# A sketched-attention and Fourier-mixing kernel: rows folded fourfold, a rearranged last group and a new instruction order

## The chip, the cores and the metric

The kernel runs on one core of a Trainium2 chip. The metric is the device time of one execution in microseconds (us); lower is better. Five engines work from queues of their own and meet only at semaphores: TensorE (PE, matmuls, with a separate row PEld for its weight loads), VectorE (DVE), ScalarE (ACT), GpSimd (POOL) and SyncE (SP, which issues nearly all transfers between memory and the core).

## The reference, cut to what matters

Two parts follow each other. The first is linear attention with a polynomial sketch for 4 batches, 4 heads, 1088 rows and a head width of 32:

```
phi(x) = (S1 x) outer (S2 x)            # 8 x 8 = 64 features
kv = sum over rows of phi(k) * v ;  z = sum over rows of phi(k)
x  = (phi(q) kv) / (phi(q) z + 1e-6)    # heads side by side: 1088 rows of 128
```

The second mixes the result with a Fourier transform and a small network:

```
u   = x + real(fft over 128 columns of fft over 1088 rows of x)
un  = (u - mean) / sqrt(var + 1e-6)     # per row
out = u + relu(un @ w_ch1) @ w_ch2      # 128 -> 512 -> 128, output float32
```

## The kernel before, in words

**Steps and order.** The kernel is a list of named steps. Each has an engine, the tiles it reads and writes, and its banks of the accumulator memory (PSUM, eight banks of 512 floats per partition). The string `ORDER` writes out by hand in which order all steps are issued, and so the order on every engine's queue. `ENGINE` moves single steps to another engine than their default, `FILL` puts matmuls on zeros ahead of a step, `BEHIND` lets a load wait for an earlier load, `AFTER` makes one step wait for another, and `BANK` gives each use its bank.

**Attention, per batch b.** `ld_k`, `ld_v` and `ld_q` load. `kT` and `qT` transpose blocks of 32 on DVE. `kpr` (L361) projects k on PE, `kab` copies on ACT, `kp` multiplies to features on POOL or DVE, `vc` copies v, `kv` (L395) sums features times v on PE, and `kvz` copies the result to SBUF. For the query, `qf` (L435) projects on PE in two halves, `qa` (ACT) and `qp` (DVE, L446) make the features, `pnd` (L481) multiplies with `kvz`, and `den`, `rden`, `x` (L490 to L496) divide. The 64 rows per head beyond 1024 go through small tiles of their own (`kt_`, `qt_`, `vt`).

**The row transform, per batch.** Partition p and slots 0 to 7 of `x{b}` hold four consecutive rows of each half of the sequence, and slot 8 holds the leftover rows. `dfold` adds and subtracts column c and column 128 - c. `fold` adds and subtracts the two halves of the sequence. `srow` (L521) multiplies with tables of cosines and sines (`tab`, `tabl`, made from phases on POOL and DVE by `turn`, `rest`, `size` and on ACT by sine), in five groups of six matmuls. `zev` takes the half spectrum out of PSUM, `zrev` makes the mirrored half with signs, `zlast` picks the columns of the leftover rows.

**The mixer, per group g of 512 rows.** Groups 0, 1, 2, 3, 5, 6, 7 and 8 are main groups, two per batch; 4 and 9 hold the leftover rows of two batches each. `mix` (L574, L577) adds x and the column transform in PSUM. `bn` and `var` take the variance on DVE, `sd` (L612) its root on ACT, `rc` the reciprocal, `un` (L623) the scaled rows. `xt` (L635) transposes them by a transfer for groups 0 to 6, and `tr` and `ut` do so through PE and a copy for 7 to 9. `ph` (L643) is the hidden layer in two halves, `rl` (L650 on ACT, L652 on DVE) the relu, `po` (L657) the second layer, summed onto u in the same bank. `fin` copies to SBUF and `out` stores. Group 8 (`TWO`) is spread over two banks and stored in two halves.

Of the kernel before, what the change touches and what calls it, by code (L numbers as in the profile page):

```python
# [12 lines left out]
I32 = mybir.dt.int32  # L13
# [9 lines left out]
LAST = HALF - 512  # L23
QD = DM // 2
NK = HALF // 2 + 1
NB = NK // 2 + 1
BY_DMA = (0, 1, 2, 3, 4, 5, 6)
SPLIT = {}
TURNS = {"un": 5, "unT": 5, "ht": 3, "ot": 4, "st": 5, "sm": 5}
NXD = 1  # L30
WARM = 4
TWO = 8
MAGIC = float(1.5 * 2 ** 23)
# [23 lines left out]
def program(nc, T, x, bank):  # L57
# [82 lines left out]
    def ld_q(b, half):  # L140
        return [nc.sync.dma_start(view(T(f"q_in{b % 3}"), 4 * H * D * half, [[4 * D, H], [1, 4 * D]], p, n),  # L141
                                  dram(x["q"], (b * H * S + half * HALF + 4 * p) * D, [[4 * D, n], [S * D, H], [1, 4 * D]]))
                for p, n in parts(f"ld_q{b}.{half}", 128)]

    def ld_qt():

        return [nc.sync.dma_start(view(T("qt_in"), 0, [[D, B * H], [1, D]], 32 * par + 16 * half, 16),  # L147
                                  dram(x["q"], (512 + HALF * half + par) * D, [[2 * D, 16], [S * D, B * H], [1, D]]))
                for par in range(2) for half in range(2)]
# [31 lines left out]
    def c_iota():  # L181
        first = nc.gpsimd.iota(T("pi")[:], pattern=[[0, 1]], base=0, channel_multiplier=1)

        nc.gpsimd.iota(T("sr")[:], pattern=[[1, 6]], base=0, channel_multiplier=4,
                       allow_small_or_imprecise_dtypes=True)
        return first
    add("c_iota", POOL, "", "iota", c_iota)

    def c_kk():
# [55 lines left out]
    add("t_cos1", ACTE, "phb/1 phb/2 phb/3 tabsin", "tab/C1", lambda: sin(
        view(T("tab"), 2 * W, [[4 * W, 2], [NB, 2], [1, NB]]), view(T("ph"), 2 * W + NB - 2, [[W, 2], [NB + 1, 2], [-1, NB]]), S))
# [24 lines left out]
    def d_trig():  # L271
        for c in range(2):
            lo, hi = slice(QD * c, QD * c + QD), slice(QD - QD * c, 2 * QD - QD * c)
            nc.scalar.activation(out=T("wd")[lo, c, :], in_=T("dpm")[lo, :], func=ACT.Sin, scale=-2 * PI / DM, bias=T("hpi")[lo, 0:1])
            nc.scalar.activation(out=T("wd")[hi, c, :], in_=T("dph")[hi, :], func=ACT.Sin, scale=-2 * PI / DM)
    add("d_trig", ACTE, "dphb dpm hpi tabsin", "wd0", d_trig)

    def d_alt(engine):

        done = []  # L280
        for c in range(2):
            p = QD - QD * c
            for i in range(2):
                done.append(memset(engine, view(T("wd"), DM * c + i, [[2, QD]], p, 1), 1.0 - 2 * i))
# [617 lines left out]
```

## Time and profile before

| what | value |
|---|---|
| median of 3 runs | 82.4 us (82.08 to 84.12) |
| the profiled execution | 82.32 us |
| its span in the profile | 80.4 us |
| busy PE, DVE, ACT, POOL | 69.6, 65.0, 49.5, 45.2 us |
| granted PE clock | 1.00 |
| read and written | 7.22 MB and 2.23 MB |

The span runs from the first to the last recorded work; the profiled execution's own time is 1.92 us longer. A busy share is a mean over stages with different limits, so the table of busy time by stage and the chain of work that ended last are read beside it. Idle time of an engine that sets nothing costs nothing.

### The profile page before, as it was taken

The numbers are of one execution on the slowest core, as the hardware profiler recorded it, in microseconds if no ns is written. First come the engines' busy times: TensorE is split into PE (matmuls) and PEld (weight loads), VectorE is DVE, ScalarE is ACT, GpSimd is POOL, SyncE is SP. The second block draws the span as 40 slices with busy tenths as digits, with TensorE's granted clock in tenths as the row PEclk, the third lists the DMA queues.
The fourth block names the chain that finished last, engine by engine and source line by source line (L and its number), as shares of the span: only waits on it lengthen the run. The fifth ranks groups of instructions, "written<-read, shape, count | busy, mean of one in ns | idle before, by whom it ended". The sixth has DMA issues, their size and how long they took to land.

```text
span 80.4 us, 3294 instructions
## 1 busy us (share of the span) xinstructions
PE 69.6 (87%) x1368; PEld 52.0 (65%) x1375; DVE 65.0 (81%) x178; ACT 49.5 (62%) x85; POOL 45.2 (56%) x84
## 2 busy tenths in 40 slices
PE   4998693799999999999999999989997969797930
PEld 2323552489799766878788789956674837583720
DVE  5895879999869999999759699999878659894800
ACT  6244576475693645479692285609978548979530
POOL 6888579975857499597999619149850010000000
PEclk9999999999999999999999999999999999999999
DMA  0969998379929659556015003030500466133042
GB/s 8 270 174 269 229 288 208 53 208 229 227 44 310 207 144 292 151 125 212 0 34 43 0 8 65 8 65 0 177 19 16 95 190 253 29 130 138 24 176 90
DMA packets 16095, 10.47 MB, mean 130 GB/s; under 512 B 6864, under 2 KB 14544, under 8 KB 16080
## 3 DMA queue, kind: packets, MB, share of 16 engines
q1 hardware_dynamic: 15896, 10.13, 47.0%
q8 instruction: 10, 0.16, 0.8%
q10 hardware_dynamic: 184, 0.14, 0.5%
q14 instruction: 5, 0.04, 0.2%
HBM read 7.22 MB, written 2.23 MB: 117 GB/s over the span
## 4 chain that ended last, share of the span: by engine, by line
PE 48%; DVE 18%; DMA 11%; SPq 8%; ACT 7%; issue 4%; DVEq 0%; ACTq 0%
PE ps L481 9%; PE ps L395 8%; PE ps L435 7%; PE ps L657 6%; DMA t_qt_in<-in_q_dram 6%; PE ps L643 5%; DMA t_unT__166<-t_un__161 5%; PE ps L361 4%; SPq L141 3%; ACT t_ht__168 L650 3%; PE ps L521 2%; PE ps L458 2%; SPq L147 2%; DVE t_x__130 L496 2%; DVE t_x__131 L496 2%
## 5 line engine op out<-in xcount | busy, mean ns | idle before, releaser
L102 POOL TENSOR_TENSOR t_kp__119<-t_ab__117 128x512 f32<-128x512 f32 x7 | 7.3, 1068 | 1.5 <-ACT t_ab__117 L413 1.1
L650 ACT ACTIVATE t_ht__167<-ps 128x1024 bf16<-128x1024 f32 x6 | 6.0, 1022 | 1.6 <-PE ps L481 1.6
L102 POOL TENSOR_TENSOR t_kp__118<-t_ab__116 128x512 f32<-128x512 f32 x6 | 6.3, 1069 | 1.0 <-ACT t_ab__116 L413 1.0
L442 ACT COPY t_qa__122<-ps 128x1024 f32<-128x1024 f32 x4 | 4.1, 1013 | 3.1 <-DVE t_qp__124 L446 1.9
L650 ACT ACTIVATE t_ht__168<-ps 128x1024 bf16<-128x1024 f32 x4 | 4.1, 1024 | 2.9 <-PE ps L577 1.9
L442 ACT COPY t_qa__123<-ps 128x1024 f32<-128x1024 f32 x4 | 4.1, 1014 | 2.3 <-PE ps L435 2.3
L643 PEld LDWEIGHTS <-t_w1b 128*128 128x128 bf16 x40 | 3.0, 97 | 3.7 <-issue 1.5
L90 PE MATMUL ps<-t_wz 128*128 128x512 bf16 x12 | 5.0, 526 | 0.0
L481 PEld LDWEIGHTS ps<-t_kvz,t_qp__124 128*64 128x64 f32 x128 | 4.0, 137 | 0.9 <-ACT t_kvz L95 0.4
L481 PE MATMUL ps<-t_kvz,t_qp__124 128*64 128x66 f32 x128 | 4.4, 223 | 0.1
L395 PE MATMUL ps<-t_v__121,t_kp__119 128*64 128x33 f32 x128 | 4.3, 223 | 0.1
L102 POOL TENSOR_TENSOR t_eo__133<-t_xd__132 128x516 bf16<-128x516 bf16 x4 | 4.2, 1052 | 0.4 <-DVE t_xd__132 L102 0.3
L395 PEld LDWEIGHTS ps<-t_v__121,t_kp__119 128*64 128x64 f32 x128 | 4.1, 138 | 0.4 <-POOL t_zl__143 L96 0.4
L395 PE MATMUL ps<-t_v__120,t_kp__118 128*64 128x33 f32 x128 | 4.3, 223 | 0.0
L481 PEld LDWEIGHTS ps<-t_kvz,t_qp__125 128*64 128x64 f32 x128 | 3.9, 137 | 0.5 <-issue 0.4
L481 PE MATMUL ps<-t_kvz,t_qp__125 128*64 128x66 f32 x128 | 4.2, 223 | 0.0
L395 PEld LDWEIGHTS ps<-t_v__120,t_kp__118 128*64 128x64 f32 x128 | 4.1, 138 | 0.1
L650 ACT ACTIVATE t_ht__169<-ps 128x1024 bf16<-128x1024 f32 x4 | 4.0, 1027 | 0.0
L652 DVE TENSOR_SCALAR t_ht__168<-ps 128x1024 bf16<-128x1024 f32 x2 | 2.5, 1225 | 1.7 <-PE ps L657 1.0
L435 PE MATMUL ps<-t_qT__115,t_sa 32*64 32x256 f32 x64 | 2.8, 400 | 1.2 <-DVE t_qp__124 L446 1.2
L379 DVE STREAM_TRANSPOSE t_kT__112<-t_k_in__105 128x512 f32<-128x512 f32 (+1 forms) x3 | 2.7, 886 | 1.1 <-DMA t_k_in__105<-in_k_dram 1.1
L361 PE MATMUL ps<-t_sblk,t_kT__112 128*64 128x64 f32 x64 | 2.5, 226 | 1.1 <-DVE t_kT__112 L379 1.1
(266 smaller groups left out, 216.6 us busy)
## 6 DMA issues: line engine op xcount, KB each, us to landing
t_q_in__109<-in_q_dram SPq DMA_DIRECT2D x4, 256.0 KB, 3.3
t_v_in__107<-in_v_dram SPq DMA_DIRECT2D x8, 128.0 KB, 3.6
t_k_in__106<-in_k_dram SPq DMA_DIRECT2D x2, 512.0 KB
t_v_in__108<-in_v_dram SPq DMA_DIRECT2D x8, 128.0 KB, 3.3
t_k_in__105<-in_k_dram SPq DMA_DIRECT2D x2, 256.0 KB
t_q_in__110<-in_q_dram SPq DMA_DIRECT2D x2, 256.0 KB, 6.6
t_q_in__111<-in_q_dram SPq DMA_DIRECT2D x2, 256.0 KB
t_k_in__105<-in_k_dram SPq DMA_DIRECT2D x1, 512.0 KB
```

The lines of the kernel that those rows point to most:

```text
L90: nc.tensor.matmul(T("ps")[:, free, :], w[:, 0:128], bass.AP(tensor=w.tensor, offset=w.offset, ap=[list(w.ap[0]), [0, 4], [1, 128]]), star ...
L102: return (nc.vector if engine == DVE else nc.gpsimd).tensor_tensor(out=out, in0=in0, in1=in1, op=op)
L361: nc.tensor.matmul(ps(use, 64 * t, [[1, 64]], 64 * c, 64), view(src, 128 * t + 64 * c, [[1, 64]]), T("sblk")[:], start=True, stop=True, ti ...
L379: nc.vector.transpose(view(T(f"kT{b % 2}"), 128 * lo, [[1, 128 * n]]), view(T(f"k_in{b % 2}"), D * lo, [[D, n], [8 * D, 4], [1, D]]))
L395: nc.tensor.matmul(ps(f"kv{b}", 33 * pr, [[1, 33]], 64 * c, 64), kp, v, start=(t == 0), stop=(t == 8), tile_position=(0, 64 * c), skip_gro ...
L435: nc.tensor.matmul(ps(f"q{b}.{pr}", 512 * g + 256 * w, [[1, 256]], 64 * h, 64), view(T(src), 0, [[1, F]], 32 * g, 32), view(T(f"qT{b % 2}" ...
L442: nc.scalar.copy(T(f"qa{pr}")[:], ps(f"q{b}.{pr}", 0, [[512, 4], [1, 256]]))
L481: nc.tensor.matmul(ps(f"nd{b}", 512 * (s // 3) + 132 * (s % 3) + 66 * pr, [[1, 66]], 64 * c, 64), w, view(T("kvz"), 132 * b + 66 * pr, [[1 ...
L496: nc.vector.tensor_tensor(out=view(T(f"x{b}"), 0, [[384, 3], [32, 12], [1, 32]]), in0=ps(f"nd{b}", 0, [[512, 3], [33, 12], [1, 32]]), in1= ...
L643: nc.tensor.matmul(ps(use, 128 * n * i, [[1, 128 * n]]), T("w1b")[:, 128 * c:128 * c + 128], own("unT", g)[:, 0:128 * n], start=True, stop ...
L650: nc.scalar.activation(out=out, in_=in_, func=ACT.Relu)
L657: nc.tensor.matmul(ps(u, ut_at(g, t), [[1, 128]]), view(own("ht", g), (128 if g % 5 == 4 else 512) * c + 128 * t, [[1, 128]]), T("w2b")[:, ...
```

## The change

The rows are laid out anew: partition p of a half holds two neighbouring rows, and partitions 64 to 127 of a q load start 288 rows further on. Even and odd slots hold rows that mirror each other about the middle of the sequence, so a new step `mfold` adds and subtracts them before `dfold`, and `dfold` and `fold` work on half as many slots. `srow` then needs three groups of six matmuls. To get the mirrored order, the query projection reads its columns in another, partly reversed order, and the mixer uses a reversed identity (`jdb`) and a table with signs (`wd` with a second half, made by `d_neg`). Two phase tables are made in place of four; ACT mirrors them (`t_far`). A main group is stored as two blocks of 256 rows with 1 KB per packet.

Group 8 (`LATE`) is no longer scaled ahead of its hidden layer: `un8` copies u as it is, `uc8` keeps u in float32, `po8` starts banks of its own, and `fin8` multiplies its sum by the reciprocal deviation and adds u. (A positive scale per row can be taken through the relu.) Order, engines, fillers, added waits and banks are new throughout.

```diff
-TURNS = {"un": 5, "unT": 5, "ht": 3, "ot": 4, "st": 5, "sm": 5}
+TURNS = {"un": 5, "unT": 5, "ht": 3, "ot": 4, "st": 5, "sm": 5, "uc": 1}
+LATE = (8,)
+FINE = ()
...
     def ld_q(b, half):
-        return [nc.sync.dma_start(view(T(f"q_in{b % 3}"), 4 * H * D * half, [[4 * D, H], [1, 4 * D]], p, n),
-                                  dram(x["q"], (b * H * S + half * HALF + 4 * p) * D, [[4 * D, n], [S * D, H], [1, 4 * D]]))
-                for p, n in parts(f"ld_q{b}.{half}", 128)]
+        return [nc.sync.dma_start(view(T(f"q_in{b % 3}"), 4 * H * D * half, [[4 * D, H], [1, 4 * D]], 64 * far, 64),
+                                  dram(x["q"], (b * H * S + half * HALF + (FAR if far else 1)) * D,
+                                       [[4 * D, 64], [S * D, H], [1, 4 * D]])) for far in range(2)]
...
-    for i, t in enumerate((0, 2, 1, 3)):
+    for a in range(2):
+        add(f"t_turn{a}", POOL, "rows kk", f"pha/{a}", lambda a=a: turn(T("ph")[:, a, :], a, base(), S))
+        add(f"t_ph{a}", DVE, f"pha/{a} rows", f"phb/{a}", lambda a=a: rest(T("ph")[:, a, :], a, base()))
...
-    add("t_neg", eng("t_neg", DVE), "tab/S0 tab/S1 tab/C0 tab/C1", "neg", lambda: t_neg(eng("t_neg", DVE)))
...
+    def c_x9(e):
+        return [memset(e, T(f"x{b}")[:, 9, :], 0.0) for b in range(B)][0]
...
     def qfeat(b, pr):
...
-                        view(T(f"qT{b % 2}"), 128 * (2 * pr + h), [[512, 2], [1, 128]], 32 * g, 32),
+                        view(T(f"qT{b % 2}"), 128 * (2 * pr + h) + (127 if g > 1 else 0),
+                             [[512, 2]] + [[-s if g > 1 else s, n] for s, n in ((32, 2), (1, 32), (64, 2))], 32 * g, 32),
...
+    def mfold(b, engine, w):
+        X = T(f"x{b}")
+        return tt(engine, view(T(f"xm{b % NXM}"), 5 * DM * w, [[DM, 5], [1, DM]]), view(X, 0, [[2 * DM, 5], [1, DM]]),
+                  view(X, DM, [[2 * DM, 5], [1, DM]]), (ALU.add, ALU.subtract)[w])
...
     def fold(b, engine, w):
-        return tt(engine, view(T(f"eo{b % 3}"), 12 * QD * w, [[3 * QD, 4], [1, n]]), view(X, 0, [[n, 4], [1, n]]), view(X, 4 * n, [[n, 4], [1, n]]), (ALU.add, ALU.subtract)[w])
+        return tt(engine, view(T(f"eo{b % 3}"), 6 * QD * w, [[3 * QD, 2], [1, n]]), view(X, 0, [[n, 2], [1, n]]), view(X, 2 * n, [[n, 2], [1, n]]), (ALU.add, ALU.subtract)[w])
     def srow(b):
...
-        for t in range(4):
+        for a in range(2):
+            six(lambda c, part: view(T(f"eo{b % 3}"), 6 * QD * c + 3 * QD * a + QD * part, [[1, QD]]),
...
+    def zev(b, half, engine):
+        copy(engine, view(T(f"z{b}"), 256 * half, [[128, 2], [1, 128]]),
+             ps(f"z{b}", *((512, [[-511, 2], [1, 128]]) if half == 0 else (783, [[-512, 2], [-1, 128]]))))
     def zrev(b, engine):
+        return copy(engine, view(T(f"z{b}"), 512, [[128, 4], [1, 128]]), view(T(f"z{b}"), 127, [[128, 4], [-1, 128]]))
...
     def un(u, g, n, engine):
+        if g in LATE:
+            copy(engine, view(out, 0, [[1, 128 * n]]), ps(u, 0, [[1, 128 * n]]))
+            return
...
     def fin(u, g, lo, hi, engine):
+        if g in LATE:
+            for t in range(lo, hi):
+                nc.vector.scalar_tensor_tensor(
+                    out=own("ot", g)[:, 128 * t:128 * t + 128], in0=ps(u, 128 * (t - lo), [[1, 128]]), scalar=own("sm", g)[:, t:t + 1],
+                    in1=own("uc", g)[:, 128 * t:128 * t + 128], op0=ALU.mult, op1=ALU.add)
+            return
...
+    def st(b, half, g, ws):
+        row = ((1, HALF + 1), (HALF + FAR, FAR))[half]
+        w, n = ws[0], len(ws)
+        return [(nc.sync, nc.scalar)[g == TWO and w == 1].dma_start(
+            dram(x["out"], (b * S + row[w]) * DM, [[2 * DM, 128], [(row[1] - row[0]) * DM, n], [1, 2 * DM]]),
+            view(own("ot", g), 256 * w, [[256, n], [1, 256]]))]
...
+    "c_v11": "DVE", "c_eo2": "DVE", "c_mask": "DVE", "c_vt0": "DVE", "c_sgn": "DVE", "vc0": "DVE", "t_far1": "ACT",
+    "t_far0": "ACT", "vc1": "ACT", "mf0.1": "DVE", "den1": "ACT", "kp2.3": "DVE", "vc2": "ACT", "vc3": "ACT", "w2b":
+    "ACT", "kp3.0": "DVE", "mf2.1": "DVE", "fin0": "ACT", "un4": "ACT", "un2": "ACT", "mf3.0": "DVE", "df3.1": "DVE",
+    "fin1": "ACT", "fin4": "ACT", "var6": "POOL", "z3.0": "DVE", "un8": "ACT", "var8": "POOL", "var7": "POOL", "ut9":
+    "DVE", "ut8": "DVE", "fin5": "ACT", "rl9.0": "DVE", "ut7": "DVE", "rl8.1": "DVE", "fin9": "ACT", "rl7.0": "DVE",
+    "fin6": "ACT", "rl8.0": "DVE", "fin7": "ACT",
...
-    "warm": (1, 1, 6), "qf0.1": (0, 2, 6), "qf0.0": (0, 3, 6), "kpr1": (0, 1, 7), "po8.0": (0, 1, 0),
+    "s_t": (0, 2, 0), "kpr0.1": (1, 1, 0), "qf0.1": (0, 1, 0), "qf1.0": (0, 2, 5), "kpr1": (1, 0, 3), "pnd0": (0, 2,
+    3), "pnd1": (0, 2, 0),
...
+    "t_turn1": "d_pm", "kp0.2": "t_pm", "kp1.3": "vc0", "kp1.2": "l_pm", "df0.1": "mf0.1", "mf2.0": "mf2.1", "mf3.1":
+    "mf3.0", "df3.0": "df3.1",
...
+c_wz warm ld_k0.0 c_bias c_v11 c_eo2 a_sin c_id ld_s1 ld_s2 s_t c_x9 c_iota c_mask c_kk c_rows c_more c_vt0 c_idb
+c_xd0 ld_k0.1 t_turn0 kT0.0 c_sgn c_cen c_jdb d_turn d_ph d_pm ld_q0.1 kT0.1 s_use kpr0.1 ld_q0.0 c_qtp kpr0.0 d_trig
...
+out4 bn8 mix7 uc8 po3 rc9 un9 ph5.1 rl5.1 var8 bn7 var7 fin3 tr9 ut9 out3 sd7 tr8 ut8 rc7 un7 ph9.0 ph6.0 rl6.0 po5
+fin5 tr7 ph8.1 rl9.0 po9 ut7 ph6.1 rl8.1 fin9 ph7.0 rl6.1 ph7.1 ph8.0 po6 rl7.0 out9 sd8 rl7.1 po7 fin6 rc8 rl8.0
+po8.0 fin8.0 po8.1 fin7 out5 out6 out7 fin8.1 out8.0 out8.1
```

More of the change, by code (lines that the diff above doesn't have):

```diff
@@ L22 @@
 ROWS = S // 32
[L23 removed]
+FAR = 288
 QD = DM // 2
@@ L858 @@
-rl0.0 bn2 var2 pnd3 eo2.0 sd2 rc2 s2 den3 rden3 x3 un2 z2 mix3 ph1.0 bn3 xt2 var3 po0 fin0 out0 rl1.0 sd3 ph1.1 ph2.0
-rc3 un3 rl1.1 rl2.0 df3.0 zr2 df3.1 eo3.1 mix5 bn5 var5 zl2 ph2.1 rl2.1 po1 mix4 eo3.0 mix6 bn4 var4 sd5 po2 sd4 rc5
-fin1 fin2 xt3 ph3.0 rl3.0 rc4 un4 un5 xt4 ph3.1 bn6 var6 sd6 rc6 xt5 un6 s3 z3 xt6 rl3.1 ph4.0 po3 zr3 rl4.0 ph5.0
-rl5.0 po4 fin3 zl3 ph5.1 fin4 mix9 bn9 mix7 ph6.0 var9 rl5.1 sd9 bn7 out2 out3 out1 out4 rl6.0 var7 rc9 po5 un9 ph6.1
-sd7 fin5 rc7 mix8 rl6.1 tr9 un7 ut9 ph9.0 tr7 rl9.0 po6 bn8 var8 ut7 sd8 rc8 fin6 ph7.0 rl7.0 un8 po9 out5 ph7.1 rl7.1
@@ L863 @@
[L863 removed]
+c_wz warm ld_k0.0 c_bias c_v11 c_eo2 a_sin c_id ld_s1 ld_s2 s_t c_x9 c_iota c_mask c_kk c_rows c_more c_vt0 c_idb
+c_xd0 ld_k0.1 t_turn0 kT0.0 c_sgn c_cen c_jdb d_turn d_ph d_pm ld_q0.1 kT0.1 s_use kpr0.1 ld_q0.0 c_qtp kpr0.0 d_trig
+qT0.1 ld_kt t_turn1 l_turn ld_q1.1 ld_vt0 qT0.0 ld_q1.0 t_ph0 ld_k1 t_ph1 t_pm ld_qt c_vt1 ld_v0.0 ld_v0.2 ld_v0.1
+ld_v0.3 kab0 kp0.2 ld_vt1 qf0.1 ld_v1.0 kt_T c_eo0 qa0.1 qT1.1 qf0.0 qa0.0 ld_q2.0 kp0.1 c_eo1 qp0.1 kt_pr kt_ab qT1.0
@@ new lines @@
+w1c zl0 kpr3 qp2.0 vc2 kab3 kp3.2 kp3.1 qf3.0 bn0 var0 sd0 kp3.3 mf1.0 kv2 df1.0 qa3.0 rc0 un0 w1b xt0 qp3.0 mix1 bn1
+var1 kvz2 vc3 w2b eo1.0 pnd2 kp3.0 den2 ph0.0 rden2 sd1 rc1 x2 kv3 eo1.1 ph0.1 un1 mf2.1 rl0.0 s1 mf2.0 rl0.1 kvz3
+z1.1 z1.0 zr1 po0 fin0 zl1 mix4 bn4 var4 sd4 mix2 xt1 bn2 var2 sd2 rc4 un4 xt4 pnd3 df2.0 df2.1 eo2.0 eo2.1 ph1.1 rc2
+rl1.1 un2 ph1.0 rl1.0 den3 rden3 x3 mix3 s2 mf3.0 z2.0 bn3 var3 sd3 ph4.0 mf3.1 df3.1 zl2 xt2 rc3 un3 po1 z2.1 mix5
+bn5 df3.0 rl4.0 po4 ph2.0 out0 xt3 zr2 eo3.1 fin1 fin4 mix6 var5 rl2.0 eo3.0 sd5 bn6 ph2.1 rc5 un5 out1 var6 rl2.1 s3
```

325 lines of the change are left out of this document (171 added, 154 removed).

## The prediction

> **What bounds the kernel now.** I read the page's busy shares first, then the chain that ended last, then a table of busy time by stage, cut where that chain changes its engine, and last the timeline of the end.
>
> The page's first part says that no engine is full over the whole span, and that TensorE (PE) and VectorE (DVE) are closest:
>
> ```profile
> PE 69.6 (87%) x1368; PEld 52.0 (65%) x1375; DVE 65.0 (81%) x178; ACT 49.5 (62%) x85; POOL 45.2 (56%) x84
> ```
>
> The table by stage (start:end, length, busy us of PE, PEld, DVE, ACT, POOL, clock, DMA share, GB/s) shows five different limits:
>
> ```profile
> 0.00:15.17 15.17, 11.15 (x149) 5.10 (x150) 12.04 (x39) 7.36 (x14) 12.17 (x35) 1.00 0.80 195
> 15.17:40.32 25.15, 25.00 (x686) 20.71 (x688) 23.25 (x38) 16.82 (x28) 19.03 (x30) 1.00 0.62 174
> 40.32:53.15 12.83, 12.17 (x287) 10.75 (x289) 11.09 (x33) 7.14 (x14) 7.73 (x11) 1.00 0.17 25
> 53.15:65.24 12.09, 10.50 (x129) 7.90 (x131) 9.73 (x40) 8.92 (x14) 6.30 (x10) 1.00 0.29 69
> 65.24:77.14 11.90, 10.76 (x117) 7.50 (x119) 8.89 (x31) 8.86 (x14) 0.00 (x0) 1.00 0.34 123
> 77.14:80.40 3.26, 0.00 (x0) 0.00 (x0) 0.00 (x0) 0.37 (x1) 0.00 (x0) 1.00 0.46 161
> ```
>
> Until 15.2 us loads and constants set the pace. From 15.2 to 40.3 PE is full (25.00 of 25.15). From 40.3 to 53.2 the chain goes qa2.0, qp2.0, pnd2, den2, x2, den3, x3, mostly on DVE. Then it goes through normalisation and a transposing DMA, and from 65.2 through PE, ACT and DVE in turn. The granted clock is 1.00 everywhere. The chain itself (start, length, engine, what, line):
>
> ```profile
> 31.44 1.08 PE ps L361 x32
> 32.52 1.76 PE ps L521 x30
> 34.29 1.05 PE ps L435 x32
> ...
> 45.74 1.37 DVE t_x__130 L496
> ...
> 61.13 4.07 DMA t_unT__166<-t_un__161
> ...
> 73.37 0.44 DVE t_unT__164 L96
> 73.80 0.05 issue
> 73.85 1.10 PE ps L643 x4
> 74.95 0.89 PE ps L657 x16
> 75.84 0.22 PE ps L90
> 76.06 0.01 issue
> 76.06 1.08 PE ps L657 x16
> 77.14 0.02 issue
> 77.17 0.37 ACT t_ot__173 L95
> ```
>
> The reader is to see that only the first sequence transform (L521 at 32.52) lies on the chain; the other three ran under the waits at 40.3, 51.1 and 61.1. At the end PE waits for the last group's normalised rows (0.44 on DVE) before its last hidden layer.
>
> **The change part by part.** The profiled execution took 82.32 us with a span of 80.4, so 1.92 lie around it; it is 0.08 under the median of 82.4.
>
> *The transform (srow).* 30 matmuls become 18 per batch of the same width. 1.76/30 is 0.059 us each, so 0.70 per batch and 2.8 of PE work in all. Counted: the first, 0.70; the other 2.1 go into waits that the chain has anyhow, and come back only if PE binds there. The leftover rows' mixL issues 2 matmuls fewer each (0.05 each by "0.20 x4" in the chain): 0.1. A zero matmul at 75.84 goes, but four new ones stand before pnd0 and pnd1 (0.22 to 0.32 each); they run while ACT copies kvz (two of 0.21), which pnd has to wait for; without that cover they cost 1.0.
>
> *Folding.* Each batch gets two sums over row pairs (mfold, 640 wide), while dfold and fold halve. On POOL 567 wide took 1.265 and 516 wide 1.05, so 640 is 1.43, 315 is 0.70 and 258 is 0.55: per batch 4.9 becomes 5.6. Three mfolds are on DVE (0.45 to 0.55 for 567; I take 0.52). The cover: x0 was ready about 6 us before s0, and the later transforms stand further from their x in the new order. Without it, 0.7 per batch.
>
> *Spectrum and tables.* Two reversed copies on ACT (0.38 each for 256 of the 512 that take 0.58) replace one of 0.79; the mirror is one POOL copy (0.61, the w2b row) in place of two signed ones (2 x 1.05 POOL, 2 x 0.59 ACT, 2 x 0.39 DVE); four small PSUM reads on DVE per batch (0.1 to 0.2 each) replace the old zlast. Two phase tables of four go (0.93 POOL, 0.50 DVE each), the sign table too (0.89 DVE), and ACT makes the far halves (2 x 0.6). With the moved steps (vc0, rl7.0, rl8.0, fin2, fin3 to DVE; vc2, fin0, fin7, kvz2, w2b to ACT; three variances of five small operations to POOL) I sum DVE at 2 us less, ACT at 0.4 less, POOL at 2 more. None of it is a term of its own.
>
> *Loads.* Every q load is two transfers of 64 partitions, and ld_qt has five: 9 more issues on SP, at 0.45 and a gap of 0.05, so 4.5 us of SP's queue. Behind them stand the k and v loads; by the instruction order at most eight transfers are open, since each waits for the eighth before it. By the old rate (about 200 GB/s to 15 us) v0 is complete near 17 instead of before 16. [...]
>
> *The start, walked by instruction order and these durations.* POOL makes the identity and pads first, so the row constants come about 1 us later, and k is transposed before q. I get kab0 at 8.6 (was 10.46). kp0.2 now waits on POOL for t_pm on DVE (10.1; POOL is free at 9.1), and behind it stand the other kp0, kt_p and with them kv0. vc0 ends at 18.6, kv0 at 21.5. The old PE had done the same set of steps (through qf1.1) at 21.34. So nothing gained: bounds from -1.5 (kab0's lead kept) to +2 (v0 and q1 late behind the extra issues); I take 0, since both queues meet again at kv0.
>
> *The strided read.* The query projection (L435) now reads its columns 64 floats apart. No row shows a matmul that reads so. Nearest is a weight load: step 1 against step 4 of 2 bytes:
>
> ```profile
> L574 PEld LDWEIGHTS <-t_idb x9: 95/96/98, 36.3 to 68.9; 128*128 128x128 bf16 x9
> L577 PEld LDWEIGHTS <-t_z__135 x4: 113/114/114, 36.4 to 36.7; 128*128 128x128 bf16 x4
> ```
>
> That is 18% more, though this load is hidden and PE's matmuls beside it took their usual 219 ns. Bounds: nothing (f32 columns pass slowly: 0.374 us for 256 is 1.5 ns a column, against 0.75 for each of 128 bf16 weights in 96 ns), and 50% more of 1.05 in 8 steps, 4.2 us. I take nothing. [...]
>
> *Late scale.* For the last main group un8 is a copy that waits for mix8 alone, so sd8, rc8 and un8 (0.30, 0.18 and 0.69 at 71.24 to 72.47) leave the chain ahead of its transposes, and tr8, ut8, ph8 move up. Added are uc8 (ACT, 0.58, in its idle), and the last store waits for two scaled sums on DVE (0.29 each by the 128-wide L623 row) in place of one copy of 0.37: +0.2. With mix9, mix8 and po4 already done, PE has from ph5.0 on 8 ph (0.45), 4 po and po3 (0.9), po9, ph9, mix7 (0.4, 0.4, 0.55) and transposes (0.6): 10.0, where the old end took 11.9 (10.76 busy). DVE has 9.5 there and ACT 7.7, so some waits stay: the gain lies between 1.0 (10.9) and 1.9 (10.0), and I take 1.6.
>
> *Stores.* A main group is 256 packets of 1 KB instead of 128 of 2 KB. Bounds for 256 KB: 2.4 (the old store) to 3.3 (loads of 512 B). Only the last half-group ends the span, and its 1 KB packets stay, so 0; if out6 and out7 crowd it, up to +0.9. The leftovers need 3 issues of 0.62, not 4.
>
> **Sum.** 82.32 - 0.70 (s0) - 0.1 (mixL) + 0 (start) - 1.6 + 0.2 (end) = 80.1; the middle up to x3 I find even within 1 us, with two of its waits shorter (x2 near 46.3, was 47.11) and x3 no earlier, because pnd3 stands behind po0 and two mixes. I take 0.2 for it. Forecast 79.9.
>
> **The rivals.**
> 1. *PE work counts in full.* If the new order lets PE run densely after 40 us, all 2.8 count, and with the end at 10.0: 82.32 - 2.8 - 0.1 - 1.9 + 0.2 = 77.7. For it: PE is the busiest engine in every stage from 15 us on. Against: DVE and ACT are busy 18 to 19 us of the last 24 before the final copy, so PE meets them often.
> 2. *The start eats it.* The eight-transfer window and 9 more issues put kv0 2 us later, and PE, full afterwards, carries this to the end: 79.9 + 2 = 81.9. For it: DMA share 0.80 until 15 us, DVE and POOL 80% busy there. Against: kab0's lead.
> 3. *The strided read decides (slower).* Place: L435 in PE's full stretch. Price: 0.53 x 8 = 4.2, so 84.1; from 0.30 us a step (2.4 in all) the gain is gone. For it: the 18% row. Against: an f32 column's slow pace.
> 4. *POOL's folds set x3 to s3.* 5.6 us per batch in a row on POOL with the waits on DVE that order them; if each of s1 to s3 waits 1.4 (an mfold), 79.9 + 4.2 = 84.1. Against: POOL had 7.73 of 12.83 and 6.30 of 12.09 busy in those stages.
>
> **How the numbers follow.** Forecast 0.50 (own range 78.6 to 81.2; nine tenths of it below 80.75), rival 1 0.15, rival 2 0.14, rival 3 0.12, rival 4 0.09. About 2% (80.75 and 84.05) is what a measurement of this kernel can tell from no change. Faster by over 2%: 0.45 + 0.15 = 0.60. Within: 0.05 + 0.13 = 0.18. Slower: 0.01 + 0.12 + 0.09 = 0.22. The range holds rival 1's price with a little beyond it and reaches to rivals 3 and 4 at 84.1: 77.3 to 84.1.
>
> **What would show it.** Right: L521 at 18 matmuls and about 1.06 a step; kv0's last matmul at 21 to 22 us; L435 at 374 to 425 ns a record and 1.05 a step; from ph5.0 to the last po under 11 us, no wait of PE for ut8. Wrong: L435 steps over 1.3; kv0 ending past 23; PE waiting for POOL before L521; x3 past 55.

## The result and the profile after

The changed kernel takes 85.04 us (median of four executions, 84.33 to 85.3) against 82.24 for the kernel before on the same chip: a ratio of 1.0345, 95% interval 1.0247 to 1.0443. It is slower. The profiled execution took 84.79 us with a span of 83.0, where the one before had 82.32 and 80.4; 2.6 us of span are to be explained, and the forecast of 79.9 has to be taken apart over 4.9.

Some executions, of the kernel before too, took 1 to 6 us more than the rest; the ratios compare the others. A ratio is turned into time by 82.2 us.

The first part of the page and the table by stage, cut where the prediction cut it (start:end, length, busy us of PE, PEld, DVE, ACT, POOL, clock, DMA share, GB/s):

```profile
PE 71.7 (86%) x1326; PEld 50.3 (61%) x1326; DVE 63.2 (76%) x184; ACT 49.3 (59%) x89; POOL 49.0 (59%) x100
```

```profile
0.00:15.17 15.17, 11.80 (x141) 5.81 (x149) 12.01 (x44) 7.06 (x14) 11.68 (x35) 1.00 0.75 161
15.17:40.32 25.15, 24.65 (x614) 18.23 (x603) 21.00 (x35) 15.13 (x25) 17.71 (x29) 1.00 0.71 185
40.32:53.15 12.83, 12.45 (x302) 9.88 (x288) 8.39 (x30) 7.96 (x16) 9.92 (x14) 1.00 0.17 43
53.15:65.24 12.09, 10.44 (x165) 7.74 (x166) 10.05 (x48) 8.12 (x18) 7.22 (x15) 1.00 0.27 69
65.24:77.14 11.90, 10.20 (x106) 6.67 (x104) 9.88 (x28) 9.76 (x16) 2.46 (x11) 1.00 0.29 80
77.14:83.01 5.87, 2.17 (x39) 1.99 (x36) 1.90 (x5) 1.28 (x3) 0.00 (x0) 1.00 0.52 179
```

PE has 42 instructions fewer and yet 2.1 us more busy time. DVE has 1.8 us less (2 were summed), and POOL 3.8 more (2 were summed). DMA moves less until 15 us: 161 GB/s, where it was 195. After that, the table does not tell more than that PE is still full; the chain does. This is the chain that ended last, up to the first transform (start, length, what):

```profile
2.15 0.75 SPq L145
...
4.26 4.63 DMA t_q_in__110<-in_q_dram
...
9.60 0.62 SPq L145
10.25 0.60 SPq L126
...
11.87 1.42 SPq L152
...
14.60 0.40 SPq L130
...
19.34 0.61 SPq L145
...
22.21 3.69 DMA t_v_in__109<-in_v_dram
25.91 0.60 SPq L145
26.56 4.57 DMA t_q_in__110<-in_q_dram
31.22 0.71 DVE t_qT__116 L453
...
33.42 1.37 DVE t_x__130 L524
...
34.93 1.09 PE ps L555 x15
```

The chain of the kernel before left the loads at 12.5 us and ran over PE from 15.2 on:

```profile
7.98 4.48 DMA t_qt_in<-in_q_dram
12.54 0.79 issue
13.32 0.68 DVE t_qtT L452
14.01 1.12 DVE t_qp__124 L446
15.17 1.65 PE ps L458 x32
```

In the changed kernel it is SP issuing loads (L145 the queries, L152 ld_qt, L130 v, L126 k) and loads landing, one after the other, for 31 us. From 15 us on PE is 98% busy beside it, which is why the shares hide it.

Milestones of both profiles. The last column leaves out the work that the new order moves across a milestone: w1c (1.13 us) from before s0 to behind it; po0 and mix4 (1.07 and about 0.75) from behind x3 to before it; po3 (0.9) from before ph5.0 to behind it; mix8, mix9 and po4 (1.2 together) from behind ph5.0 to before it. Also s2 (1.25), which ran while x3 was waited for, now runs behind x3, and ph1.0 and ph1.1 (0.9) the other way:

| stretch | before | after | difference | without moved work |
|---|---|---|---|---|
| to the end of kv0 and qf1.1 | 21.35 | 22.79 | +1.44 | +1.4 |
| to the end of s0 | 12.94 | 13.38 | +0.44 | +1.6 |
| to the end of x3 | 18.81 | 21.27 | +2.46 | -0.5 |
| to the start of ph5.0 | 12.14 | 10.39 | -1.75 | -0.6 |
| to the end of the last po | 11.89 | 11.48 | -0.41 | -0.1 |
| to the end of the span | 3.27 | 3.69 | +0.42 | +0.4 |

The last column adds up to 2.2 us; the other 0.35 of the 2.6 is s2 against ph1. So 3.0 us are lost before 36 us, in the start and between kv0 and s0, about 1 us is won back up to ph5.0, and what was to be won at the end did not come.

### The profile page after: what moved, and what is told of

The parts are those of the page before. It is cut to its first block, busy times and chain, and to the rows that moved or that the text cites. A ratio compares the mean times of both kernels' runs of the same rounds, so it can differ in the third digit from the quotient of the medians.

```text
span 83.0 us, 3251 instructions
## 1 busy us (share of the span) xinstructions
PE 71.7 (86%) x1326; PEld 50.3 (61%) x1326; DVE 63.2 (76%) x184; ACT 49.3 (59%) x89; POOL 49.0 (59%) x100
## 4 chain that ended last, share of the span: by engine, by line
PE 33%; SPq 19%; DMA 16%; DVE 15%; ACT 6%; issue 4%; POOL 2%; DVEq 0%; ACTq 0%
DMA t_q_in__110<-in_q_dram 11%; SPq L145 8%; PE ps L509 6%; PE ps L420 5%; PE ps L681 5%; DMA t_v_in__109<-in_v_dram 4%; SPq L152 4%; PE ps L697 4%; SPq L130 4%; PE ps L460 3%; PE ps L555 3%; ACT t_ht__164 L688 2%; PE ps L607 2%; POOL t_xm__133 L105 2%; DVE t_x__130 L524 2%
## 5 line engine op out<-in xcount | busy, mean ns | idle before, releaser
L105 POOL TENSOR_TENSOR t_kp__120<-t_ab__118 128x512 f32<-128x512 f32 x7 | 7.3, 1067 | 4.0 <-DVE t_v__121 L99 2.4
L105 POOL TENSOR_TENSOR t_kp__119<-t_ab__117 128x512 f32<-128x512 f32 x7 | 7.4, 1065 | 2.1 <-DVE t_pm L231 2.1
L105 POOL TENSOR_TENSOR t_xd__134<-t_xm__133 128x315 bf16<-128x315 bf16 x7 | 5.4, 782 | 3.3 <-DVE t_xm__133 L105 3.0
L688 ACT ACTIVATE t_ht__164<-ps 128x1024 bf16<-128x1024 f32 x5 | 5.0, 1021 | 3.0 <-PE ps L681 2.9
L93 PE MATMUL ps<-t_wz 128*128 128x512 bf16 x14 | 5.6, 506 | 1.0 <-DVE t_less L184 1.0
L688 ACT ACTIVATE t_ht__165<-ps 128x1024 bf16<-128x1024 f32 x4 | 4.1, 1028 | 1.2 <-PE ps L681 1.2
L688 ACT ACTIVATE t_ht__166<-ps 128x1024 bf16<-128x1024 f32 x4 | 4.1, 1021 | 0.6 <-PE ps L681 0.6
L386 PEld LDWEIGHTS ps<-t_sblk,t_kT__113 128*64 128x64 f32 x64 | 2.8, 181 | 1.9 <-DVE t_sblk L369 1.4
L460 PE MATMUL ps<-t_qT__115,t_sa 32*64 32x256 f32 x64 | 3.2, 448 | 0.6 <-DVE t_qT__115 L453 0.6
L98 ACT COPY t_kvz<-ps 64x66 f32<-64x66 f32 x8 | 1.7, 207 | 3.3 <-PE ps L420 3.2
L460 PE MATMUL ps<-t_qT__116,t_sa 32*64 32x256 f32 x64 | 3.6, 452 | 0.0
```

What stands on the lines that cost most here:

```text
L93: nc.tensor.matmul(T("ps")[:, free, :], w[:, 0:128], bass.AP(tensor=w.tensor, offset=w.offset, ap=[list(w.ap[0]), [0, 4], [1, 128]]), star ...
L105: return (nc.vector if engine == DVE else nc.gpsimd).tensor_tensor(out=out, in0=in0, in1=in1, op=op)
L460: nc.tensor.matmul(ps(f"q{b}.{pr}", 512 * (0, 1, 3, 2)[g] + 256 * w, [[1, 256]], 64 * h, 64), view(T(src), 0, [[1, F]], 32 * g, 32), view( ...
L688: nc.scalar.activation(out=out, in_=in_, func=ACT.Relu)
```

## The experiments

Three causes offered themselves: the strided read of the queries (A), fillers and order that put pnd right behind kv (B), and the query loads in halves (C). The first four runs take one away each, and then all three.

**e1_plain_read.**
```
-  [[512, 2]] + [[-s if g > 1 else s, n] for s, n in ((32, 2), (1, 32), (64, 2))]
+  [[512, 2], [1, 128]]
```


> The changed kernel (85.04 us, 1.0345 of the kernel before) with one edit: the query feature matmuls read their moving operand in the old pattern, two runs of 128 neighbouring elements, instead of 2 x 32 x 2 elements that lie 32 and 64 apart and run backwards for half of the groups. The rows then come out in another order than the output needs; the work is otherwise the same. Theory A, the pattern of the read: a matmul of this line falls from 429-432 ns a record to about 374-400 and a step from 1.27 to 1.05 us; eight steps lie in stretches where PE is never idle, so 1.6-1.7 us come off, 83.4 us, ratio about 1.014. Theory B, the order and the fillers, and theory C, the query loads in halves: the steps still get shorter only if the pattern matters, and if PE's late start and waits set the time, at most 0.5 us come off, 84.5 us or more.

Ratio 1.0202 (1.0128 to 1.0276), 1.2 us less than the changed kernel. The steps came down from 1.34 to 1.12 us, from first start to last end. In the profile kv0 starts 0.4 us sooner and s0, pnd3, the last po and the end 0.8, 1.1, 1.1 and 1.1. Theory A holds, with 1.1 to 1.2 of the expected 1.6: of the four steps ahead of kv0 half is lost, since PE waits in their place for kpr1's operand (0.8 us).

**e2_no_fill.**
```
-FILL ... "kpr1": (1, 0, 3), "pnd0": (0, 2, 3), "pnd1": (0, 2, 0)
+FILL ...
```


> The changed kernel without the filler matmuls ahead of kpr1 (one float32, 1.06-1.12 us), pnd0 and pnd1 (two bfloat16 each, about 0.6). The fillers compute nothing that is used. Theory B, that they lie on PE's path: 0.34 us before kpr1 (its operand comes 0.7 us after the filler starts) and 0.2 to 0.6 us at each pnd (the copy that they cover takes 0.43 us, so 0.2 beyond it, or all of it if the copy is not waited for): 0.5 to 1.2 us off, 83.8 to 84.5 us. Theories A (the pattern of the read) and C (the loads): no more than 0.3 us, 84.7 to 85.1. A rival to B: the granted clock is 1.0 with them and falls without them; then the kernel gets no faster or slower.

Ratio 1.0214 (1.0144 to 1.0284), 1.1 us less, though the interval overlaps that of the changed kernel. Its profile is of its longest execution (85.57 us) and shows no gain at kv0, which starts at 20.72 us: PE waits 0.67 and 0.53 us at pnd0 and pnd1, and 1.54 for kpr1's operand, where the fillers stood. Where the 1.1 us come from is thus not shown.

**e3_q_single.**
```
-  ... 64 * far, 64), dram(... + (FAR if far else 1)) * D, [[4 * D, 64], ...])) for far in range(2)]
+  ... dram(x["q"], (b * H * S + half * HALF + 1) * D, [[4 * D, 128], [S * D, H], [1, 4 * D]]))]
```


> The changed kernel with each load of queries as one transfer of 128 partitions instead of two of 64; the second 64 partitions then hold the rows that follow, so the rows that are computed are others than the output needs, while every size stays. The SP waits point at the same transfers as before. Theory C, that eight more issues (0.5 us each, 4 of them ahead of the first v load) hold up v0: the v0 loads are issued about 2 us sooner, vc0's input lands near 17.0 instead of 18.95, and kv0 starts 1 to 2 us sooner than 20.50; 1.0 to 1.5 us off, 83.5 to 84.0 us. Theories A (the read's pattern) and B (order and fillers): PE is full from 15 us on, so an earlier v0 changes only PE's wait ahead of kv0; 0 to 0.4 us off, 84.6 to 85.0.

Ratio 1.0107 (1.0063 to 1.0151), 2.0 us less, the largest of the three. The v0 loads are issued from 11.13 us (14.60 in the changed kernel), and kv0 starts at 18.84 (20.50). The changed kernel, then e3_q_single:

```profile
20.50 1.13 PE L420 MATMUL ps<-t_v__121,t_kp__119 128*64 128x33 f32 x32
```

```profile
18.84 1.13 PE L419 MATMUL ps<-t_v__121,t_kp__119 128*64 128x33 f32 x32
```

The 1.7 us at kv0 are 2.1 at the start of s0 and 1.9 at the end of the span. Theory C holds, and its rival, that a full PE would swallow the gain, falls. With single transfers the steps through kv0 and qf1.1 end at 21.13 us, as early as in the kernel before (21.35).

**e4_all_three.** The three edits together.

> The three edits together: plain read in the query features, no fillers ahead of kpr1, pnd0 and pnd1, and each load of queries as one transfer (the rows that come out are not the output's). If the three causes add up: 1.6 + 0.8 + 1.0, 3.4 us off, 81.6 us, below the kernel before (ratio 0.99). If they lie beside each other (PE waits in place of the work that is taken away): 1.6 to 2.0 us off, 83.0 to 83.4. If something else in the order sets the time: over 84.

Ratio 1.0048 (0.998 to 1.0116): 2.4 us less than the changed kernel, so the three do not add up to 4.3, and what is left of the change, with all that its order costs, is worth nothing. The waits of PE between 15 and 58 us show one reason (who waits, for whom, us in total, times, longest):

```profile
PE ps L507 <- ACT t_kvz L98: 1.2, 2, 0.7
PE ps L679 <- ACT t_ht__165 L686: 1.1, 1, 1.1
PE ps L385 <- DVE t_kT__114 L403: 0.8, 1, 0.8
...
```

L507 is pnd: without fillers, pnd0 and pnd1 wait 0.7 and 0.5 us for the copy of kvz. The fillers there, 0.61 each, only stand in a wait that the order makes; L385 is kpr1, which waits 0.8 for its operand where the filler takes 1.1. By these waits the fillers cost about 0.3 (1.1 less 0.8), and the order 1.2. This is not the 1.1 of e2_no_fill; which of the two holds for the fillers stays open, and no run changed the place of pnd alone.

**b1_strided and b2_split**: the same two edits, done to the kernel before.
```
b1:  -  [[512, 2], [1, 128]]
     +  [[512, 2]] + [[-s if g > 1 else s, n] for s, n in ((32, 2), (1, 32), (64, 2))]
b2:  -SPLIT = {}
     +SPLIT = {f"ld_q{b}.{half}": (64, 64) for b in range(4) for half in range(2)}
```


> The kernel before (82.3 us) with one edit: its query feature matmuls read their moving operand in the new pattern (2 x 32 x 2 elements, 32 and 64 apart, backwards for half of the groups). Rows come out in another order than the output needs; nothing else changes. Theory A, that the pattern costs about 0.2 us of each of eight steps: seven of the steps lie where PE is full, so 1.1 to 1.6 us more, 83.4 to 83.9 us, ratio 1.013 to 1.02, with each step at 1.25 to 1.3 instead of 1.12 us. Rival, that the long steps of the changed kernel come from its order (reads of one bank, writes into others): the steps stay at 1.12 and the time within 0.3 us.

> The kernel before with each load of queries as two transfers of 64 partitions; the same rows, the SP waits on the same transfers. Theory C, that the extra issues hold up what is behind them on SP: four of them stand ahead of the last three v0 loads, which are issued 2 to 3 us later than 9.56-12.38, and kv0 starts 1 to 2 us later than 18.05: 83.3 to 84.3 us, ratio 1.012 to 1.025. Rival, that the kernel before has slack there (its v0 loads are issued 2 us sooner than the changed kernel's): under 0.5 us more.

b1_strided: 1.0142 (1.0042 to 1.0242), 1.2 us more, steps at 1.35. b2_split: 1.0372 (1.0252 to 1.0492), 3.1 us more, over what was expected; its profiled span is 81.9 us, 1.5 over the kernel before, and a further 1.0 of that execution lies outside the span. In the profile x3 ends 1.6 us later and PE runs at a granted clock of 0.5 from 17.3 to 20.7 us; as another execution at a mean clock of 1.00 took 85.58 us, how much of the loss is the clock stays open. Both causes are the change's own, not its order's.

**e5_head_pairs**: as many query transfers as in the changed kernel, cut the other way.
```
-  ... 64 * far, 64), dram(..., [[4 * D, 64], [S * D, H], [1, 4 * D]])) for far in range(2)]
+  ... 4 * H * D * half + 8 * D * i, [[4 * D, 2], [1, 4 * D]]), dram(..., [[4 * D, 128], [S * D, 2], [1, 4 * D]])) for i in range(2)]
```


> The changed kernel with each load of queries still as two transfers, but of 128 partitions and two heads each instead of 64 partitions and four heads; the rows are those of the single transfer of the run before, so others than the output needs. If the number of issues is what holds up v0: as the changed kernel, kv0 near 20.5, 84.5 to 85.0 us. If it is that a transfer of 64 partitions is slower: as with single transfers, kv0 near 18.8, 83.0 to 83.3 us.

Ratio 1.0138 (1.0078 to 1.0197), as with single transfers (1.0107) within the noise. So it is mostly not the number of issues. At kv0 they do show:

```profile
19.45 1.12 PE L420 MATMUL ps<-t_v__121,t_kp__119 128*64 128x33 f32 x32
```

This lies between 18.84 and 20.50: about 0.6 of the 1.7 us is the count of the issues, 1.05 the cut along the partitions. The first four query issues, at the same place on SP (start, length together, line, count), for the changed kernel and then for e5_head_pairs:

```profile
2.15 2.72 SPq L145 DMA_DIRECT2D t_q_in__110<-in_q_dram  x4
```

```profile
2.16 2.04 SPq L145 DMA_DIRECT2D t_q_in__110<-in_q_dram  x4
```

With the gaps between them, a transfer of 64 partitions and four heads takes 0.68 us of SP on average, one of 128 partitions and two heads 0.51, for the same bytes in the same 512-byte pieces; it lands after a median of 4.4 us in place of 3.7 (the eight into t_q_in__110). In e5_head_pairs the chain to s0 runs over PE again:

```profile
19.52 2.25 PE ps L420 x72
21.85 0.21 ACT t_kvz L98
...
22.42 2.33 PE ps L509 x72
24.75 1.27 PE ps L460 x32
26.02 2.22 PE ps L420 x72
...
33.46 1.24 PE ps L555 x18
```

Why the transfer over half of the partitions is the slower one no trace here shows.

**b3_patterns**: which part of the pattern costs.
```
-  [[512, 2], [1, 128]]
+  ([[512, 2], [32, 2], [1, 32], [64, 2]], [[512, 2], [-1, 128]], [[512, 2], [1, 64], [64, 2]], [[512, 2], [1, 2], [2, 64]])[b]
```


> The kernel before, with another read of the queries in each batch (rows then come out in other orders than the output needs): batch 0 reads 2 x 32 x 2 elements forwards with a step of 64 elements innermost; batch 1 reads 128 neighbours backwards; batch 2 reads 64 pairs with a step of 64, without the 32-element level; batch 3 reads with a step of 2 elements. Its steps are read from the trace against 1.12 us in the kernel before. If the step of 256 bytes is what costs: batches 0 and 2 at 1.25 to 1.35, batch 1 at 1.12, batch 3 at or near 1.12. If it is the direction: batch 1 at 1.25 or more, 0 and 2 at 1.12. If it is any read that is not of neighbours: batches 0, 2 and 3 alike at 1.25 to 1.35.

One step of each batch, in the order of the batches (start, length of the 16 matmuls, tiles, [wait before]):

```profile
10.40 0.80 PE L435 MATMUL ps<-t_qT__114,t_sa 32*64 32x256 f32 x16
10.98 0.75 PE L435 MATMUL ps<-t_qT__114,t_sb 32*64 32x256 f32 x16
...
13.31 0.69 PE L435 MATMUL ps<-t_qT__115,t_sa 32*64 32x256 f32 x16 [1.57 <-DVE t_qp__124 L448]
13.79 0.64 PE L435 MATMUL ps<-t_qT__115,t_sb 32*64 32x256 f32 x16
...
26.25 0.79 PE L435 MATMUL ps<-t_qT__114,t_sa 32*64 32x256 f32 x16
26.84 0.74 PE L435 MATMUL ps<-t_qT__114,t_sb 32*64 32x256 f32 x16
...
30.99 0.72 PE L435 MATMUL ps<-t_qT__115,t_sa 32*64 32x256 f32 x16
31.50 0.66 PE L435 MATMUL ps<-t_qT__115,t_sb 32*64 32x256 f32 x16
```

Steps: 1.33 us with 64 elements between neighbours, 1.12 backwards, 1.33 without the 32-element level, 1.17 with a step of 2 elements. The distance costs; the direction and the extra level do not. Steps between 2 and 64 were not run. The price was 0.21 us or 19% of a step at a distance of 64 elements and still 0.05 us at 2; why, these runs do not tell.

**e6_x3_early and e7_x3_banks**: is x3's late place (57.44 us, 53.10 before) a cost of its own? The heart of the two edits:
```
e6:  s1 mf2.0 kvz3 rl0.1 pnd3 z1.1 z1.0 zr1 po0 fin0 zl1 ... den3 rden3 x3 mf3.0 ... mix4 ... mix2     nd3=3 h0.1=5
e7:  kvz3 mf2.0 ... pnd3 rl0.1 s1 den3 rden3 x3 mf3.0 z1.1 z1.0 ... po0 fin0 zl1 mix2 ... mix4         nd3=3 h0.1=0
```


> The changed kernel with pnd3, den3, rden3 and x3 moved ahead of po0, mix4 and mix2 on PE and of their statistics on DVE; nd3 takes banks 3 to 5 in place of 0 to 2, and h0.1 bank 5 in place of 3, so that pnd3 need not wait for the reads of z1. Theory D, that x3's place in the order keeps 1 to 2 us: pnd3 starts near 50.9 instead of 53.1, x3 ends near 55.3 instead of 57.4, and s3 near 63 instead of 64.5: 83.5 to 84.3 us. Rival, that DVE and ACT have the same work to do before s3 either way (mix4's and mix2's statistics then come later): x3 is earlier, s3 is not, 84.7 to 85.3 us.

> The changed kernel with pnd3, den3, rden3 and x3 again ahead of s1's reads, po0, mix2 and mix4, and the banks mended: nd3 has banks 3 to 5, and h0.1, which takes two banks, has 0 and 1 (in e6_x3_early it had 5 and 6, and bank 6 still held group 0). Theory D, that x3's late place keeps time: pnd3 starts near 50.2, x3 ends near 54.5 instead of 57.4, s3 starts at 61.5 to 62 instead of 63.2, 1.0 to 1.7 us off: 83.3 to 84.0 us. Rival: what was moved behind x3 (the statistics of groups 2 and 4, the reads of z1) then stands before s2 and s3 on DVE and ACT; s3 stays within 0.5 us of 63.2 and the time within 84.5 to 85.5.

Ratios 1.0626 (1.0553 to 1.0698) and 1.0965 (1.0845 to 1.1085). x3 came 2.4 and 1.9 us sooner, at 55.04 and 55.58, and s3 started 2.6 and 5.7 us later, at 65.87 and 68.97. The rival holds, in a stronger form: PE waited 2.3 and 3.2 us in one piece for ht at ph1.0, because rl1.1 stands on ACT behind the scaling of group 4 (in e7 of groups 2 and 4), whose statistics now came behind x3 on DVE. Both times lie outside what either theory gave. Neither version keeps the reference's output (in e6, h0.1 is given bank 6 while that still holds group 0), so they are read for time alone. What the gap then set off shows in e7_x3_banks, cut at 3.41 us, the time that the granted clock stayed at 0.50 in e6_x3_early (58.95 to 62.37):

```profile
55.99:59.40 3.41, 1.13 (x11) 0.49 (x9) 2.50 (x17) 1.66 (x7) 2.68 (x3) 1.00 0.00 0
59.40:62.82 3.42, 2.00 (x9) 0.95 (x10) 0.10 (x1) 2.32 (x4) 0.00 (x0) 0.50 0.21 42
62.82:66.23 3.41, 3.41 (x32) 2.68 (x29) 2.16 (x15) 0.97 (x5) 0.99 (x2) 0.50 0.60 88
66.23:69.64 3.41, 3.17 (x39) 2.31 (x38) 2.75 (x15) 3.14 (x7) 2.07 (x5) 1.00 0.35 95
```

PE was busy for 1.13 of 3.41 us, and for the next 6.8 the granted clock (third from the end) was 0.50, which is part of the loss. x3's place is thus no loss that a move alone gets back; that another arrangement of banks could was not shown.

**e8_scale_early**: the late scaling by itself.
```
-  un8 bn9 var9 out2 sd9 ph5.0 rl5.0 out4 bn8 mix7 uc8 ... var8 ... sd8 ... rc8
+  bn8 var8 bn9 var9 out2 sd8 rc8 un8 sd9 ph5.0 rl5.0 out4 mix7 uc8        AFTER "un8": "rc8"
```


> The changed kernel, with the copy un8 of the last main group made to wait for that group's statistics (bn8, var8 on DVE, sd8, rc8 come ahead of it), as a group that is scaled at this place must; the sum is still scaled at the end, so the banks and the work are the same. If the late scaling is worth the 1.6 us that were forecast: 1 to 1.6 us longer, 86 us or more. Theory E, that it is worth little in this order, because tr8 waits till 71.4 us for its bank, which fin3 still reads, while un8 is done at 68.7: un8 then ends near 70.5 to 71, tr8 still starts near 71.4, and the time stays within 0.3 us of 85.0.

Ratio 1.049 (1.0127 to 1.0853). The one execution at full clock took 85.75, 0.7 over the changed kernel; the others 87.0 to 87.6, with 3.41 us at half clock (72.9 to 76.3 in the profile, after a stretch with PE busy 1.16 of 3.41). Theory E falls: tr8's bank is not what is late, but rl5.0 and with it ph5.1, which stand on ACT behind sd8 and un8; PE waits 1.9 us for them. The edit also moves var8 from POOL to DVE. The 0.7 us rest on one execution, against 84.33 to 85.3 of the changed kernel, so what the late scaling is worth at this place is not firmly shown; with un8 set behind rl5.0 it may be less, and that was not tried.

**e9_v0_first, e10_v0_fill, e11_dve_order, e12_both**: can the start and the read be mended with the output kept?
```
e9:   ld_v0.* ahead of ld_qt; vc0 ahead of qt_T; kpr1 kv0 qt_f qf1.1 pnd0; FILL without kpr1, pnd0
e10:  e9, FILL "kpr1" back, ld_vt1 ahead of ld_qt, l_ph l_pm ahead of qt_p
e11:  for c in range(2): nc.vector.transpose(view(qT, 512 * half + c, [[64, 8], [2, 32]]),
                                             view(q_in, 512 * half + 64 * c, [[128, 4], [32, 2], [1, 32]]))
      and the read  [[512, 2], [-1 if g > 1 else 1, 128]]
```


> The changed kernel in another order at the start, with the same rows and the same two transfers for each load of queries: the four v0 loads stand ahead of the five ld_qt transfers on SP, vc0 ahead of qt_T on DVE, and kv0 ahead of qt_f and qf1.1 on PE, so that pnd0 no longer stands right behind kv0 and its wait for kvz0 is covered; the fillers ahead of kpr1 and pnd0 are left out. Theory C and theory B together (v0 too late on SP, pnd0 right behind kv0): v0 lands 3 us sooner, kv0 starts near 17.5, and pnd0 ends near 24.3 instead of 25.8; 1.2 to 1.6 us off, 83.4 to 83.8 us. Rival: the sum of the loads up to 25 us is what sets the start (q2, q3 and v1 come no sooner), and the gain is lost at kv1 or at s0: 84.5 to 85 us.

> e9_v0_first with the filler ahead of kpr1 put back (one float32 matmul of 1.1 us, in a wait for kT1 of 1.8), the two ld_vt1 transfers also ahead of ld_qt (kv0 waited for them, to 18.74), and l_ph and l_pm ahead of qt_p on DVE. In e9_v0_first PE was busy for 0.47 of the 3.41 us before 18.05, and the granted clock was 0.5 for the 10.24 us after that. If it was that gap that cost 3 us there, the clock stays at 1.0 here, kv0 starts near 18.2, pnd0 ends near 25.0 instead of 25.8, and the time is 84.2 to 84.9 us. If the loads up to 26 us set the start whatever the order, kv1 waits for v1 and the time is that of the changed kernel, 84.8 to 85.3. If the order itself was bad, it stays over 86.

> The changed kernel, with the rows put in the folded order by DVE: each qT transpose is two of half the size, which write every second element, and the query feature matmuls then read neighbours (backwards for half of the groups). The output is the reference's. Theory A: the steps take 1.12 instead of 1.27 to 1.34 us, as in e1_plain_read, at the price of eight more DVE instructions in time that DVE has: 0.8 to 1.2 us off, 83.8 to 84.2 us, ratio about 1.02. Rival: the strided write is as dear on DVE as the read was on PE (a transpose of 512 elements 0.70 us now; two of 256 over 1.0 together), and DVE passes it on to qp1.0 and x1: under 0.4 us off.

> e10_v0_fill and e11_dve_order together; the output is the reference's. If the causes that remain are the ones named (half-partition transfers are still there, the read and part of the wait for v0 are mended): 1.3 to 1.8 us off, 83.2 to 83.7 us, ratio 1.01. If the start is bound by the loads: as e11_dve_order, 83.8 to 84.2.

e9_v0_first took 86.15 to 89.86 us. In its profile, cut again at 3.41 us, PE fell to 1.59 busy (waits of 1.8 us for kT1, where the filler was left out, and 0.7 for qtT), and 10.24 us at half clock followed:

```profile
14.63:18.05 3.42, 1.59 (x48) 1.01 (x32) 2.05 (x3) 1.16 (x2) 2.02 (x3) 1.00 0.34 54
18.05:21.46 3.41, 2.72 (x52) 2.75 (x53) 1.71 (x2) 0.58 (x1) 1.06 (x1) 0.50 0.64 159
21.46:24.87 3.41, 3.41 (x56) 3.35 (x57) 0.00 (x0) 0.42 (x2) 0.00 (x0) 0.50 0.64 172
24.87:28.29 3.42, 3.42 (x58) 2.59 (x52) 1.93 (x6) 1.39 (x2) 0.00 (x0) 0.50 0.86 256
28.29:31.70 3.41, 2.47 (x84) 2.16 (x88) 3.29 (x7) 2.90 (x5) 3.12 (x3) 1.00 0.80 237
```

The execution of 86.15 had a mean clock of 0.996, so the gap did not cost the clock each time. e10_v0_fill kept the clock at 1.0 and still came to 1.0584 (1.0512 to 1.0656): the third case. kv0 starts 1 us sooner (19.51), but qf2.1 at 28.09 instead of 25.73, because qT2 stands on DVE behind qp1.1, which now comes later. The changed kernel's order was the better one for loads that arrive this late; SP's queue was not shortened by it. e11_dve_order: 1.0311 (1.0203 to 1.0419), 0.3 us less. The steps are back at 1.12, but two transposes of 256 that write every second element take 0.76 us from start to end (0.41 to 0.43 each) where one of 512 took 0.70, and PE then waits 0.8, 0.6 and 0.5 us for vc1, x1 and qT2: with the loads as late as they are, the read is hardly worth mending. e12_both: 1.0489 (1.0347 to 1.063), e10's loss less a little. No version here beats the kernel before.

## Why the prediction was wrong, by its own steps

**The start, taken as 0: +1.4 us, carried to the end.** This step failed first. "By the old rate v0 is complete near 17": vc0 waited for it until 18.95. The extra issues were counted, but at 0.45 and a gap of 0.05; a query transfer over 64 partitions took 0.61 to 0.75, and ld_qt's five took 0.42 to 1.42 behind them. Rival 2 named this, with 2 us and a chance of 0.14. Its reason was half right: at kv0 about 0.6 us is the count of the issues, 1.05 that the transfers span half of the partitions (e5); in the kernel's time the halves are 1.7 to 2.0 us (e3, e5). The forecast of kv0's end, 21.5, would have been right with single transfers (21.13 in e3); it was 22.79. That the transfers over half of the partitions landed later than those over all of them in e5 (a median of 4.4 us against 3.7) is not in the sum, and the row for query loads in the kernel before (t_q_in__109, 256 KB, 3.3 us from issue to landing), which shows only whole loads, could not have shown it.

**The strided read, taken as 0: 1.7 us of PE, 1.2 of the time.** Rival 3's mechanism, at 0.21 to 0.22 a step and not 0.53, so under the 0.30 from which it was to decide. The nearest row, the weight load with a step of 8 bytes, said 18% more, and the steps took 19% more; as the queries' step is 256 bytes, and one of 8 bytes cost 4% here (b3), that agreement is luck. The upper end (0.53, 50% of a step) was the author's assumption, which no row and no run shows; 0.21 to 0.22 came in its place. The argument that a float32 column passes slowly enough was the wrong ground for preferring the lower bound.

**The fillers, hidden: nearly so, but the wait they hide was not counted.** pnd right behind kv waits 0.7 and 0.5 us for kvz when they are left out (e4), and where they stand they fill that time. In the old order qf1.1 stood between kv0 and pnd0. These 1.2 us are missing from the sum. What the fillers cost by themselves stays open (1.1 by e2's time, 0.3 by e4's waits).

**The transform, -0.70 at s0: right.** From first start to last end 1.94 became 1.24. The other three can't be read one by one: from s0 to ph5.0 the stretches are 1.1 us shorter without moved work, and s2, now on PE's path, takes 0.35 of it back against ph1.

**The middle, -0.2: about right, -0.5 up to x3,** though x3 at 57.44 passed the mark of 55: 1.8 us of it is work moved ahead of x3, and the rest came from the 3.0 us lost before s0's end. For x3 to ph5.0 the sum has no term, yet the sum of the end counts mix8, mix9 and po4 (1.2 us) as done by then: that is a term put at nothing.

**The end, -1.6 + 0.2: it brought 0.** From ph5.0 to the last po 11.5 us, not 10.3 (11.9 before); mis-sized by 1.2. PE was busy for 10.3 of it, where 10.0 were summed, and waits 1.2 for DVE and ACT, which were busy 11.74 and 11.05 us of the 14.84 from s3 to the last po: 0.9 alone for bank 0, which fin3 read behind bn7 on DVE. So 0.3 is more work and 0.9 waiting that the sum of PE's work left out. The tail is 0.42 longer, most likely as out6, out7 and both halves of out8 are issued within 3 us.

**Rivals 1 and 4** did not come: PE waited for POOL at no transform, and 0.2 us for ACT at s3. One mfold on POOL (1.41 us from 58.12) does lie on the chain between x3 and s3.

The steps put together afterwards, on the profiled execution: 82.32 - 0.70 (s0) + 1.4 (start) + 0.5 (two strided steps from kv0 to s0) + 1.2 (pnd behind kv) + 0.4 (vc1 and x1, waited for before kv1 and s0) - 0.5 (to x3) - 0.6 (to ph5.0) + 0.35 (s2 against ph1) - 0.1 (end) + 0.4 (tail) = 84.7; measured 84.79. Its terms are read from the table above, so that it comes close is no test of them.

## What to carry to other kernels

When a change cuts a load in two, ask along which dimension: halves along the heads cost this kernel little (kv0 came 0.6 us later, and the time stayed within the noise), halves along the partitions 1.7 to 2.0 us. Where PE is full, follow the chain and not the shares: here PE was 98% busy from 15 to 40 us, and the chain beside it was SP and DMA. A wait that another step used to cover comes back when the order removes that step; list what stood between a producer and its consumer before calling a wait hidden.

## What the runs showed of the hardware that was not expected

- A gap in PE can be paid twice. In e6, e7, e8 and e9 a stretch of 3.41 us, cut where the granted clock changed, with PE busy for 0.32, 0.33, 0.34 and 0.47 of it was followed by 3.41, 6.8, 3.41 and 10.24 us at a granted clock of 0.50. A stretch with 0.50 (b3_patterns, 11.16 to 14.58 us) was followed by a clock of 1.00. b2_split shows one case with 0.75 (13.87 to 17.28 us) that was followed by 0.50 for 3.4 us, so the busy share alone does not tell what follows. A filler in a wait can be worth its place for this: with the one ahead of kpr1 put back, beside two other edits, e10_v0_fill had PE busy for 2.21 of the 3.42 us in which e9 had 1.59, and a granted clock of 1.00 after them. It need not be, as e4_all_three kept the clock at 1.00 up to 70 us without three of them.
- Two engines that read one PSUM tile took turns. ACT's second copy of z waited 1.2 and 0.5 us for DVE's zlast of the same tile (changed kernel, 50 to 70 us):

```profile
ACT t_z__141 L98 <- DVE t_zl__143 L99: 1.2, 1, 1.2
...
ACT t_z__140 L98 <- DVE t_zl__143 L99: 0.5, 1, 0.5
```

The waits are for semaphores, so the order is the program's own; whether the two reads could have run at once was not shown. The change adds readers of z, and these waits come with them.
